# Seven half products for eight on freshly made score groups as well: seven more attention groups per batch on the cheaper scheme

## The chip, the cores and the metric

The kernel runs on one core of a Trainium2 chip. The metric is the device time of one execution in microseconds (us), the median of several runs. The engines are PE (matrix multiply; PEld is its weight load), DVE (vector), ACT (scalar), POOL (general purpose) and SP (issues transfers).

## The reference, cut to what matters

```python
# u, v: 8 x 3008 x 256; z: 8 x 3008 x 64
scores = (1/S) * z @ z.T                # per batch, symmetric
attn   = maximum(scores, 0) ** 2        # still symmetric
x      = u * (attn @ v)
h      = x @ w_in                       # 256 -> 2048
out    = (h * cos(h)) @ w_out           # 2048 -> 256
```

Of the kernel before, what the change touches and what calls it, by code (L numbers as in the profile page):

```python
# [14 lines left out]
def kernel(  # L15
# [9 lines left out]
    nc = tc.nc  # L25
    AF = mybir.ActivationFunctionType
    ALU = mybir.AluOpType
# [20 lines left out]
    NSLOT = 18  # L48
    NW = 4
    PLAN = {  # L50
        2: [(1.0, 'P1 P5'), (1.4, 'P2 B1'), (2.15, 'P6'), (2.55, 'B1'),
            (3.0, 'P3 B1'), (3.4, 'P7'), (4.15, 'B1'), (4.35, 'A1 B1'), (4.75, 'A2'),
            (5.0, 'P4 A1 B1'), (5.4, 'B1'), (6.15, 'A1 B1'), (6.35, 'A1'),
            (6.55, 'A3 B3'), (6.75, 'A3 B1'), (7.0, 'B1'), (7.4, 'A3 B2')],
        3: [(1.0, 'P1 P5 P2'), (2.55, 'P6'), (2.75, 'B2'), (3.0, 'B2'),
            (3.4, 'P3'), (4.15, 'P7'), (4.75, 'A1'), (5.0, 'P4 A1 B1'), (5.4, 'B2'),
            (6.15, 'A1'), (6.35, 'A2'), (6.55, 'A1 B2'), (6.75, 'A2'), (7.0, 'B2'),
            (7.4, 'A3')],
        4: [(0.75, 'P1 P5'), (1.0, 'P2'), (2.35, 'P6 B1'), (2.75, 'P3'),
            (3.4, 'P7'), (4.55, 'B2'), (4.75, 'P4 A1'), (5.0, 'A1 B1'), (5.4, 'A1'),  # L60
            (6.15, 'B1'), (6.35, 'A1'), (6.55, 'A3'), (6.75, 'B1'), (7.0, 'B1')],
        5: [(1.0, 'P1 P5'), (1.4, 'P2'), (2.15, 'P6'), (2.75, 'P3 B1'),
            (3.0, 'B1'), (4.15, 'P7'), (4.35, 'B1'), (4.55, 'A1'), (5.0, 'P4'),
            (5.4, 'B2'), (6.35, 'A1'), (6.55, 'A2 B1'), (7.0, 'A2 B1'), (7.4, 'A1')],
    }
    SUM1, SUM2, WADD, RADD = (-3.0, 0.5), (1.5, 0.15000000000000002), 4.56, 4.25
    CMIN, XEND = 2, 4.0
    HALF = 4.4

    inv_s = 1.0 / float(S)  # L70
    inv_s2 = inv_s * inv_s
# [154 lines left out]
    def direct(b, c, R):  # L226


        return b == 0 and c <= 2

    halves = {}
    slot_of = {}

# [2 lines left out]

    def seven(b, c):

        if c < CMIN or direct(b, c, c):
            return []  # L240
        return list(range(min(c, NW)))

    def s_matmuls(b, c, R, p):


        zt = zT[b % 2]
        banks = {}
        diagonal = R == c and (b, c) > (0, NC // 2)
        for k in ((0, 1), (3, 2) if diagonal else (2, 3))[p]:
            s0 = k if diagonal else 0  # L250
            lo = 1 if k in ((1, 2) if diagonal else (1, 3)) else 0
            h = slice(lo * dqk, (lo + 1) * dqk)
            j0 = c * K + 1 - lo
            sp = ps_w.tile([P, CW], FP32, name="w")
            chain(nc.tensor.matmul(  # L255
                sp[:, s0 * P:], zt[h, R * K + k + 1 - lo, :],
                zt[h, j0 + s0:j0 + K, :].rearrange("p j w -> p (j w)"),
                start=True, stop=True))
            banks[k] = sp
        return banks  # L260

    def s_squares(b, c, R, p, banks):
        if p == 0:
            halves[(b, c, R)] = slot("a", b, c, R)
        t = halves[(b, c, R)]
        diagonal = R == c and (b, c) > (0, NC // 2)
        rt = rpool.tile([P, 2, CW], FP16, name="rt")
        if diagonal:

            for i in range(2):  # L270
                k = 2 * p + i
                nc.scalar.activation(rt[:, i, k * P:], banks[k][:, k * P:], AF.Relu)  # L272
                nc.vector.tensor_tensor(  # L273
                    t[:, k, k:, :].rearrange("p s w -> p (s w)"),
                    rt[:, i, k * P:], rt[:, i, k * P:], ALU.mult)
                if k < K - 1:
                    nc.sync.dma_start_transpose(
                        t[:, k + 1:, k, :],
                        t[:, k, k + 1:, :].rearrange("p s w -> p (s w)"))
            if p == 1:  # L280
                fresh[(b, c, R)] = [t[:, k, :, :] for k in range(K)]
            return
        for i in range(2):
            k = 2 * p + i
            if direct(b, c, R) and (k == 3 or c == R == 0 and i):
                nc.vector.tensor_scalar_max(rt[:, i, :], banks[k], 0.0)
            else:
                nc.scalar.activation(rt[:, i, :], banks[k], AF.Relu)  # L288
        rv = rt.rearrange("p k (s w) -> p k s w", s=K)
        nc.vector.tensor_tensor(  # L290
            t.rearrange("p s k w -> p k s w")[:, 2 * p:2 * p + 2], rv, rv, ALU.mult)
        if p == 1:
            fresh[(b, c, R)] = [t[:, :, k, :] for k in range(K)]
            if R > c and not direct(b, R, c):
                tt = slot("t", b, c, R)
                turned[(b, c, R)] = tt
                nc.sync.dma_start_transpose(
                    tt.rearrange("p s k w -> p (s k) w"),
                    t.rearrange("p s k w -> p (s k w)"))
# [22 lines left out]
    def wide(b, c):  # L322
        return min(CW, S - c * CW)
# [59 lines left out]
        nc.gpsimd.tensor_tensor(o[:, 1], t[:, k2, d2], o[:, 0], ALU.subtract)  # L383
        nc.gpsimd.tensor_tensor(o[:, 3], t[:, k2, d1], o[:, 1], ALU.subtract)

    def quarter(b, c, R, kk, tk):

        h = wide(b, c) // 2
        tt = turned[(b, R, c)].rearrange("p s k w -> p s (k w)")
        return tt[:, 2 * kk:2 * kk + 2, tk * h:(tk + 1) * h]  # L390

    def second(b, c, R):
        h = wide(b, c) // 2
        t = slots[slot_of[("x", b, c)]].rearrange("p (r k h) -> p r k h", r=K, k=2)
        return t[:, R, :, 0:h]

    def a_sums1(b, c, R):
        s1 = quarter(b, c, R, 0, 1)
        after(nc.vector.tensor_tensor(s1, s1, quarter(b, c, R, 1, 1), ALU.add).ins,
              before[-1], NOSYNC)  # L400
        nc.vector.tensor_tensor(
            second(b, c, R), s1, quarter(b, c, R, 0, 0), ALU.subtract)

    def a_sums2(b, c, R):

        h = wide(b, c) // 2
        tt = turned[(b, R, c)].rearrange("p s k w -> p (s k w)")
        part = tt.ap[0]
        src = bass.AP(tt.tensor, tt.offset + 2 * CW,
                      (part, (h, 2), (CW, 2), (1, h)))  # L410
        dst = bass.AP(tt.tensor, tt.offset + h,
                      (part, (2 * CW - h, 2), (CW, 2), (1, h)))
        x = second(b, c, R)
        sub = x.unsqueeze(1).broadcast_to([P, 2, 2, h])
        after(nc.vector.tensor_tensor(dst, src, sub, ALU.subtract).ins,  # L415
              before[-1], NOSYNC)

# [2 lines left out]
    def product(b, c, n):  # L420
# [9 lines left out]
        for i, R in enumerate(W):  # L430
            j = R * K
            v0 = lambda kk, dd: vs(b, j // G)[
                :, j % G + 2 * kk:j % G + 2 * kk + 2, dd * P:(dd + 1) * P]
            lhs, rhs = {
                1: lambda: (v0(0, 0), quarter(b, c, R, 0, 0)),
                2: lambda: (v0(1, 0), quarter(b, c, R, 1, 0)),
                3: lambda: (v0(1, 1), quarter(b, c, R, 0, 1)),
                4: lambda: (vsum[R][:, 3], quarter(b, c, R, 1, 1)),
                5: lambda: (vsum[R][:, 0], quarter(b, c, R, 0, 1)),
                6: lambda: (vsum[R][:, 1], second(b, c, R)),  # L440
                7: lambda: (vsum[R][:, 2], quarter(b, c, R, 1, 0)),
            }[n]()
            for k in range(2):
                chain(nc.tensor.matmul(  # L444
                    acc[bank][:, cols], lhs[:, k, :], rhs[:, k, :],
                    start=(n in (1, 5) and i == k == 0),
                    stop=(i == len(W) - 1 and k == 1), skip_group_check=True))

# [64 lines left out]
    def at(t, rank, f):  # L513
        events.append((t, rank, len(events), f))
# [47 lines left out]
                use(("a", b, c, R), t, t + 3)  # L562
    for b in range(B):
        for R in range(NW):
            at(b * span + (2.0 + 0.5 * R if b else 2 * U + R), 2, lambda b=b, R=R: v_sums(b, R))
        for c in range(NC):
            t = b * span + c * U
            W = seven(b, c)
            d = direct(b, c, c)
            ready = 1.5 + when[(b, c, NC - 1)]  # L570
            first, last = (0.6, 6.93) if d else (HALF if W else 1.0, 7.3)
            room = [i for i, sc in enumerate(scores)
                    if max(ready, t + first) < sc[0] < t + last and i not in also]
            if room:
# [9 lines left out]
                places = [(t + q + (0.5 if q < U - 1 else -0.05), 3) for q in range(U)]  # L584
            elif W:
                for i, R in enumerate(W):
                    at(t + SUM1[0] + SUM1[1] * i, 2, lambda b=b, c=c, R=R: a_sums1(b, c, R))
                    use(("x", b, c), t + SUM1[0], t + XEND)
                    use(("t", b, R, c), t, t + 6.5)
                    at(t + SUM2[0] + SUM2[1] * i, 2.5, lambda b=b, c=c, R=R: a_sums2(b, c, R))  # L590
                at(t + WADD, 2.6, lambda b=b, c=c: keep(b, c, 0))
                at(t + RADD, 2.6, lambda b=b, c=c: keep(b, c, 8))
                done = [0, 0]
                for o, what in PLAN[c]:
                    for piece in what.split():
# [120 lines left out]
```

## The kernel before: the parts that the change and the argument touch

A batch has 24 blocks of 128 keys (the last has 64) and six *columns* of 512 queries (the last has 448). A *group* (c, R) is the attention of the four key blocks R with the queries of column c. As the scores are symmetric, a group with R > c is made once and turned by a transposing transfer for its mirror image. A column's visit takes eight *units*, about 25 us; times in the program are in units from the start of the visit or of the batch. Score matmuls, products with v and the two layers that follow are interleaved on PE by these times.

Plainly, a group costs eight matmuls of 512 columns (four key blocks times two halves of d, the 256 features of v). In the seven-product scheme the group and its v blocks are cut into 2 x 2, and seven products of sums do the work of eight: 14 matmuls of 256 columns. Sums of the attention quarters are made on DVE, sums of the v quarters on POOL, once per batch and key group. In the code, `after(x, y, NOSYNC)` only keeps the scheduler from placing x before y; nothing waits for it.

```python
def v_sums(b, R):                       # POOL; k1, k2: block pairs; d1, d2: halves of d
    o = vsum[R]
    after(nc.gpsimd.tensor_tensor(o[:, 0], t[:, k1, d2], t[:, k1, d1], ALU.subtract).ins, before[-1], NOSYNC)
    nc.gpsimd.tensor_tensor(o[:, 2], t[:, k2, d2], t[:, k1, d2], ALU.subtract)
    nc.gpsimd.tensor_tensor(o[:, 1], t[:, k2, d2], o[:, 0], ALU.subtract)
    nc.gpsimd.tensor_tensor(o[:, 3], t[:, k2, d1], o[:, 1], ALU.subtract)

def a_sums1(b, c, R):                   # DVE, both inputs in SBUF
    s1 = quarter(b, c, R, 0, 1)
    after(nc.vector.tensor_tensor(s1, s1, quarter(b, c, R, 1, 1), ALU.add).ins, before[-1], NOSYNC)
    nc.vector.tensor_tensor(second(b, c, R), s1, quarter(b, c, R, 0, 0), ALU.subtract)
# ... a_sums2: one more subtraction of twice the size, between products 6 and 7

def s_squares(...):                     # DVE, both inputs in SBUF
    nc.scalar.activation(rt[:, i, :], banks[k], AF.Relu)          # empties a PSUM bank
    nc.vector.tensor_tensor(t[...], rv, rv, ALU.mult)             # frees rt
def h_quantum(...):                     # DVE, one input in PSUM, one in SBUF
    nc.vector.tensor_tensor(gs[...], hp, c16, ALU.mult)           # empties a PSUM bank

# when (before):
at(b * span + (2.0 + 0.5 * R if b else 2 * U + R), 2, lambda b=b, R=R: v_sums(b, R))
```

Before, only turned groups (R < c) of columns 2 to 5 used the scheme: 102 groups. Score matmuls and the two layers share six PSUM work banks; PE stops when none is free.

## Time and profile before

| | before |
|---|---|
| time, median of the runs beside the changed kernel | 1231.01 us (1228.36 to 1232.28, 4 runs) |
| span of the profiled run, granted clock | 1230.2 us, 0.999 |
| PE / DVE / ACT / POOL busy | 99% / 77% / 66% / 19% |
| start to start of a matmul of 512 / 256 columns, most frequent | 0.216 / 0.109 us |
| PE time lost (see below) | 22.0 us, of which 13.0 in the first 76 us |

*PE time lost* is used throughout. It was worked out from the order of time of all PE matmuls: the time from one start to the next, less columns/2400 us and 0.0025 us; a run of matmuls of 64 rows counts half its columns, as two run side by side, and each switch between 64 and 128 rows counts 0.09 us (there are 242 of them in every run, so this choice doesn't touch the differences). What is left of the span, 1230.2 - 22.0 = 1208.2 us, is by this construction the time of the columns at full clock: it follows from the number of matmuls.

The page's first part (engine, busy us, share of the span, instructions) of the kernel before:

```profile
PE 1218.0 (99%) x8145; PEld 740.2 (60%) x8145; DVE 941.4 (77%) x1788; ACT 817.3 (66%) x1702; POOL 235.7 (19%) x329
```

From its groups of instructions, shapes kept apart (count | busy us, mean ns | idle before): the first sums on DVE, whose second half is L401, and the squares.

```profile
L290 DVE TENSOR_TENSOR s<-rt 128x1024 f16<-128x1024 f16 x254 | 178.2, 708 | 138.7 <-ACT rt L288 131.9 <-DMA s<-s 5.9
L401 DVE TENSOR_TENSOR s<-s 128x512 f16<-128x512 f16 x70 | 28.8, 420 | 1.0
L399 DVE TENSOR_TENSOR s<-s 128x512 f16<-128x512 f16 x70 | 28.6, 419 | 0.0
```

The order of time around the start of batch 4 (start, duration). First POOL of the kernel before: its v sums run from 594.27 to 602.9 us, one group after the other. Those that need the sum just made start 0.74 to 0.75 us after it, so there is a pause of 0.07 to 0.08 us before each of them (595.83 to 595.91, for one).

```profile
592.15 2.12 POOL L113 DMA_DIRECT2D v<-in_v_dram  x3
594.27 0.82 POOL L380 TENSOR_TENSOR vsum<-v 128x256 f16<-128x256 f16 x1
595.17 0.66 POOL L383 TENSOR_TENSOR vsum<-v,vsum 128x256 f16<-128x256 f16 x1
...
602.27 0.67 POOL L384 TENSOR_TENSOR vsum<-v,vsum 128x256 f16<-128x256 f16 x1
```

DVE of the same kernel in the same stretch: from 594.49 to 604.45 us it has nothing but `g` products, with one input in PSUM, and they keep their 0.69 us.

```profile
594.49 2.48 DVE L484 TENSOR_TENSOR g<-w,c 128x512 f16<-128x512 f32 x4
598.87 0.69 DVE L484 TENSOR_TENSOR g<-w,c 128x512 f16<-128x512 f32 x1 [1.91 <-ACT c L481]
...
604.45 0.69 DVE L290 TENSOR_TENSOR s<-rt 128x1024 f16<-128x1024 f16 x1 [2.28 <-ACT rt L288]
```

### The profile page before, as it was taken

The page shows a single profiled execution, that of the slowest core. Times are in us where ns is not written, and L with a number is a line of the kernel's source. Part 1 is how long each engine was busy: PE and PEld are TensorE (multiplying, and loading weights), DVE is VectorE, ACT ScalarE, POOL GpSimd, SP SyncE. Part 2 cuts the span into 40 slices and gives each one's busy share as a digit, 9 for nine tenths or more (in the row PEclk, how much of TensorE's full clock was granted, in tenths as well). Part 3 has the DMA queues.
Part 4 walks back from the last instruction along what each step waited for, and adds up shares of the span by engine and source line. Part 5 has one row for each costly group of instructions (what it writes and reads, how often), then busy time and mean ns, then how long its engine had stood idle before and what let it go on. Part 6 is the DMA issues. An engine that isn't in the chain of part 4 may idle for free.

```text
span 1230.2 us, 22337 instructions
## 1 busy us (share of the span) xinstructions
PE 1218.0 (99%) x8145; PEld 740.2 (60%) x8145; DVE 941.4 (77%) x1788; ACT 817.3 (66%) x1702; POOL 235.7 (19%) x329
## 2 busy tenths in 40 slices
PE   8999999999999999999999999999999999999998
PEld 3366555665566655666556665566655666556666
DVE  8888767886688866888678886687867878678775
ACT  6667666676676766767667676676766767666645
POOL 5610401014010150101501014010140111400000
PEclk9999999999999999999999999999999999999999
DMA  9997957689696796967969679685795857956411
GB/s 161 172 164 118 145 91 125 116 127 144 96 123 113 118 144 104 123 105 118 147 99 128 101 118 150 100 129 104 111 155 98 131 101 110 158 94 118 72 28 51
DMA packets 484221, 144.97 MB, mean 118 GB/s; under 512 B 432400, under 2 KB 484112, under 8 KB 484112
## 3 DMA queue, kind: packets, MB, share of 16 engines
q1 hardware_dynamic: 356448, 88.73, 45.2%
q0 software_dynamic: 100400, 29.77, 25.5%
q10 hardware_dynamic: 27264, 25.06, 6.4%
q8 instruction: 64, 1.05, 0.4%
q14 instruction: 45, 0.37, 0.1%
HBM read 60.29 MB, written 24.64 MB: 69 GB/s over the span
## 4 chain that ended last, share of the span: by engine, by line
PE 92%; DMA 4%; issue 1%; POOL 1%; DVE 1%; ACT 1%; POOLq 0%; DVEq 0%
PE w L494 25%; PE w L477 25%; PE acc L340 22%; PE acc L444 12%; PE w L255 6%; DMA v<-in_v_dram 4%; DMA ut<-ust 1%; PE acc L317 1%; POOL v L113 1%; POOL vsum L382 0%; DVE g L484 0%; PE w L673 0%; ACT rt L288 0%; ACT zT L218 0%; ACT c L481 0%
## 5 line engine op out<-in xcount | busy, mean ns | idle before, releaser
L481 ACT ACTIVATE c<-w 128x512 f16<-128x512 f32 x752 | 439.1, 623 | 263.3 <-PE w L477 224.8
L484 DVE TENSOR_TENSOR g<-w,c 128x512 f16<-128x512 f32 x752 | 492.4, 685 | 104.0 <-ACT c L481 101.7
L494 PE MATMUL w<-w_out,g 128*128 128x256 f16 x3008 | 448.7, 273 | 0.0
L477 PE MATMUL w<-x,w_in 128*128 128x512 f16 x1504 | 445.9, 379 | 0.0
L494 PEld LDWEIGHTS <-g 128*128 128x128 f16 x3008 | 294.2, 98 | 191.2
L340 PE MATMUL acc<-s,v 128*128 128x512 f16 (+1 forms) x1392 | 363.7, 380 | 2.2 <-DVE x L369 2.2
L288 ACT ACTIVATE rt<-w 128x512 f16<-128x512 f32 x489 | 253.2, 616 | 89.6 <-PE w L255 89.6
L290 DVE TENSOR_TENSOR s<-rt 128x1024 f16<-128x1024 f16 x254 | 178.2, 708 | 138.7 <-ACT rt L288 131.9
L340 PEld LDWEIGHTS <-v 128*128 128x128 f16 x1392 | 130.9, 98 | 130.6 <-issue 36.6
L477 PEld LDWEIGHTS <-w_in 128*128 128x128 f16 x1504 | 146.8, 98 | 66.0 <-issue 4.1
L113 POOL DMA_DIRECT2D ust<-in_u_dram x112 | 81.6, 735 | 527.6 <-PE acc L340 508.8
L444 PE MATMUL acc<-s,vsum 128*128 128x256 f16 (+1 forms) x816 | 106.0, 268 | 0.0
L255 PE MATMUL w<-zT 64*128 64x512 f16 (+3 forms) x684 | 91.6, 361 | 3.6 <-ACT zT L218 1.6
L444 PEld LDWEIGHTS <-vsum 128*128 128x128 f16 x816 | 78.9, 98 | 11.9 <-issue 1.9
L444 PE MATMUL acc<-s,v 128*128 128x256 f16 (+1 forms) x612 | 79.7, 269 | 0.0
L272 ACT ACTIVATE rt<-w 128x512 f16<-128x512 f32 (+3 forms) x176 | 63.0, 451 | 23.9 <-PE w L255 23.9
L501 ACT ACTIVATE ob<-w 128x256 f32<-128x256 f32 x188 | 71.1, 378 | 5.4 <-PE w L494 5.4
L369 DVE TENSOR_TENSOR x<-acc,ut 128x64 f16<-128x64 f32 (+7 forms) x178 | 69.4, 430 | 5.9 <-PE acc L340 3.8
L444 PEld LDWEIGHTS <-v 128*128 128x128 f16 x612 | 57.8, 98 | 13.6 <-issue 8.6
L415 DVE TENSOR_TENSOR s<-s,s 128x1024 f16<-128x1024 f16 (+1 forms) x102 | 63.6, 664 | 2.7 <-PE acc L444 2.7
L273 DVE TENSOR_TENSOR s<-rt 128x512 f16<-128x512 f16 (+3 forms) x176 | 51.0, 340 | 17.9 <-ACT rt L272 17.2
L255 PEld LDWEIGHTS <-zT 64*128 64x128 f16 x684 | 25.6, 94 | 59.8 <-issue 45.7
(38 smaller groups left out, 371.8 us busy)
## 6 DMA issues: line engine op xcount, KB each, us to landing
out_dram<-ob ACTq DMA_DIRECT2D x92, 256.0 KB, 2.3
ust<-in_u_dram POOLq DMA_DIRECT2D x80, 128.0 KB, 5.0
v<-in_v_dram POOLq DMA_DIRECT2D x16, 512.0 KB, 6.5
s<-s SPq DMA_TRANSPOSE x249, 4.6
v<-in_v_dram POOLq DMA_DIRECT2D x8, 448.0 KB, 10.3
zst<-in_z_dram POOLq DMA_DIRECT2D x14, 128.0 KB, 5.0
ust<-in_u_dram POOLq DMA_DIRECT2D x16, 96.0 KB, 4.4
w_in<-in_moe_w_in_dram POOLq DMA_DIRECT2D x4, 256.0 KB, 10.2
```

What stands on the lines that cost most here:

```text
L113: hold(nc.gpsimd.dma_start(dst, src))
L255: chain(nc.tensor.matmul(sp[:, s0 * P:], zt[h, R * K + k + 1 - lo, :], zt[h, j0 + s0:j0 + K, :].rearrange("p j w -> p (j w)"), start=True, ...
L288: nc.scalar.activation(rt[:, i, :], banks[k], AF.Relu)
L290: nc.vector.tensor_tensor(t.rearrange("p s k w -> p k s w")[:, 2 * p:2 * p + 2], rv, rv, ALU.mult)
L340: chain(nc.tensor.matmul(acc[:, 0:wn], vs(b, j // G)[:, j % G, nh * P:(nh + 1) * P], a, start=(start and n == 0), stop=(last and n == len( ...
L369: nc.vector.tensor_tensor(x[:, nh, :], acc[nh][:, o:o + n], ut[:, nh, o:o + n], ALU.mult)
L444: chain(nc.tensor.matmul(acc[bank][:, cols], lhs[:, k, :], rhs[:, k, :], start=(n in (1, 5) and i == k == 0), stop=(i == len(W) - 1 and k ...
L477: chain(nc.tensor.matmul(hp, w_in16[:, k, ft * P:(ft + 1) * P], x[:, k, :], start=(k == 0), stop=(k == NDH - 1)))
L481: nc.scalar.activation(c16, hp, AF.Sin, bias=math.pi / 2.0, scale=inv_s2)
L484: nc.vector.tensor_tensor(gs[(m, ft // FG)][:, ft % FG, :], hp, c16, ALU.mult)
L494: chain(nc.tensor.matmul(ys[m][:, 0:D], gs[(m, f4)][:, ft % FG, ts * P:(ts + 1) * P], w_out16[:, ft, :], start=(ft == 0), stop=(ft == NFT ...
L501: nc.scalar.activation(obs[m][:, i, :], ys[m][:, 0:D], AF.Copy, bias=0.0, scale=inv_s2)
```

## The change

The intent: PE does nothing but stream columns, so use the cheaper scheme for more groups. A fresh group (R > c, or on the diagonal) lies with keys and queries laid out the other way about, so its quarters are found by other strides. In every batch but the first, columns 0 to 3 now have three such groups and columns 4 and 5 four: 151 instead of 102. As column 0 now needs vsum one unit into its visit, the v sums move from 2.0 units after the batch's start to before it.

```diff
-    SUM1, SUM2, WADD, RADD = (-3.0, 0.5), (1.5, 0.15), 4.56, 4.25
-    CMIN, XEND = 2, 4.0
-    HALF = 4.4
+    SUM1, SUM2, WADD, RADD = {0: (-3.9, 0.65), 1: (-3.8, 0.35), ...}, ...
+    TSUM = [-2.0, -1.9, -0.8, 2.0, 2.5]
+    WSET = {0: [0, 1, 2], 1: [0, 1, 2], 2: [0, 1, 2], 3: [0, 1, 2], 4: [0, 1, 2, 3], 5: [0, 1, 2, 3]}
+    HALF = {0: 5.2, 1: 3.9, 2: 3.7, 3: 4.1, 4: 4.2, 5: 4.7}
...   (PLAN: the places of the products within a visit, anew for columns 0 to 5)
     def seven(b, c):
-        if c < CMIN or direct(b, c, c):
-            return []
-        return list(range(min(c, NW)))
+        return [] if direct(b, c, c) else WSET[c]
...   (quarter() becomes quarters(), which takes the strides of either layout)
-                    acc[bank][:, cols], lhs[:, k, :], rhs[:, k, :],
+                    acc[bank][:, cols], lhs[:, k, :],
+                    rhs[:, k, :] if old else rhs[:, :, k * P:(k + 1) * P],
...
-            at(b * span + (2.0 + 0.5 * R if b else 2 * U + R), 2, lambda b=b, R=R: v_sums(b, R))
+            at(b * span + (TSUM[R] if b else 2 * U + R), 2, lambda b=b, R=R: v_sums(b, R))
```

## The prediction

> **What bounds it now.** TensorE. The page shows PE busy 99% of 1230.2 us, granted clock full (0.999), DVE 77%, ACT 66%, and the chain that ended last is 92% PE. Busy is modelled for matmuls, so I read start-to-start spacing in the order of time of the PE instructions: in the steady state a 512-column matmul starts every 0.216 us and a 256-column one every 0.109 us, whatever its line. That is the "N/2.4 + 2.5 ns" of the Trainium skill, "TensorE: Matmul & The Clock Gate", section "Back-to-back issue gap" (215.8 and 109.2 ns); its "sustained" 131 ns for 512 columns is not what this trace shows. Weight loads (98 ns) hide even at 256 columns. PE's time is thus columns plus about 2.5 ns per matmul, plus few stalls. After the first 75 us the only visible ones are waits for the third v load at the start of batches 3 to 5 (chain of waits: DMA v, 4.2 us on PEld in 5 places, 1.9 us on PE, overlapping); by spacing some 2.3 us are lost.
>
> **What the change does.** Groups done with seven half products go from 102 to 151: per batch 1 to 7, column 0 gets 3, column 1 gets 3, column 2 one more (its diagonal). By the instruction order the PE loses 392 matmuls of 512 columns and gains 686 of 256; nothing else on PE changes in number, and the switches between 64-row and 128-row matmuls stay at 242.
> - PE: 392 x 0.216 - 686 x 0.1087 = 84.7 - 74.6 = **-10.1 us**, all on the critical path (0.206 us per group).
> - DVE: 49 x (0.419 + 0.420 + 0.685) for the sums, 14 x (0.424 + 0.414 + 0.690) for combining in the two newly converted columns: +96 us, 941 to about 1037, 85% of the span. ACT: 28 x 0.377 + 14 x 0.413 = +16 us, to about 834. POOL: same operations, issued earlier.
> - The windows of batch 4 show DVE 61% and 69% busy in columns 0 and 1 and 77 to 86% in columns 2 to 5, without PE stalls. After: about 85% to 90% everywhere. So most of the added DVE work lands in idle time.
> - The half-row product of column 0 moves from 1.0 to at least 5.2 eighths of its visit, and the third v group is first read near 6: the v waits should vanish (about -2 us). POOL now makes vsum before that load; it is issued some 2 to 3 us later, harmlessly.
>
> **What is given back.** DVE bursts (three or four 0.685 us subtractions together) delay the evacuations that free the six PSUM work banks, and blocks in bank 0 follow within 0.1 to 0.3 unit of an in-place add. I allow 1 to 2 us for all 48 visits.
>
> Predicted: 1230.9 - 10.1 - 2 + 1 = about **1219.8 us** (0.9% less), 8 times in 10 between 1214.5 and 1226. Chances: faster by over 2% 0.01, within 2% 0.97, slower by over 2% 0.02.
>
> **What would show the steps.** Right: matmul spacing still 0.216 and 0.109; batch period falling from 152.5 to about 151 us; batch 0 unchanged; DVE near 1037 us with per-operation means unchanged; no PE or PEld wait for v after the first batch. Wrong: PE or PEld waits for DVE (acc, x, g, s lines) of over 3 us in total, above all in columns 0 and 1; products waiting for POOL vsum at a batch's start; strided moving operands (two runs of 128) spaced wider than 0.109.
>
> **What would make it wrong.** DVE at 85 to 90% leaves little slack: if each converted visit stalls PE by 0.3 us, 48 visits return the gain entirely. A late vsum of the third group could stall each of seven batches by about 1 us.

## The result, and the profile after

| | before | after |
|---|---|---|
| time, median | 1231.01 us (4 runs) | 1267.33 us (1266.09 to 1268.61, 4 runs) |
| span, granted clock | 1230.2 us, 0.999 | 1266.8 us, 0.980 |
| PE time lost | 22.0 us | 68.3 us |
| span less PE time lost | 1208.2 us | 1198.5 us |

The ratio is 1.0298 (95% interval 1.0278 to 1.0318): 3% slower. Ratios here are the mean time of one kernel's fast runs over that of the other's fast runs of the same rounds, so not quite the ratio of the medians. The last row is worth a look first: the columns, counted at full clock, cost 9.7 us less, as forecast, and 46 us of lost PE time came on top. (That row is a count; what was measured is that the spacing stays at 0.216 and 0.109 us.)

The page after, answering to the line of before:

```profile
PE 1229.4 (97%) x8439; PEld 774.7 (61%) x8439; DVE 1057.0 (83%) x1977; ACT 836.1 (66%) x1744; POOL 237.8 (19%) x329
```

Its groups, shapes apart. L422 and L424 are the two first sums. Before, both took 0.42 us; now the second has a mean of 705 ns. The excess is 119 x (0.705 - 0.417) = 34 us.

```profile
L301 DVE TENSOR_TENSOR s<-rt 128x1024 f16<-128x1024 f16 x254 | 180.4, 717 | 102.3 <-ACT rt L299 101.1
L424 DVE TENSOR_TENSOR s<-s 128x512 f16<-128x512 f16 x119 | 83.3, 705 | 1.5
L422 DVE TENSOR_TENSOR s<-s 128x512 f16<-128x512 f16 x119 | 51.4, 437 | 0.0
```

A mean of this kind asks for the spread. The view of that one line shows a median of 416 ns and a maximum of 6365 ns:

```profile
L424 DVE TENSOR_TENSOR s<-s x151: 377/416/6365, 56.5 to 1213.5; 128x512 f16<-128x512 f16 x119, 128x448 f16<-128x448 f16 x32
```

Looked up in the order of time, seven of the 119 carry the excess: one at each of the seven batch starts, three of about 6.36 us and four of 4.50 us (there POOL's row is shorter: six sums, and a pause before the seventh of 0.33 and 0.50 us in two batches and of 0.01 to 0.02 us in the other two). Here is DVE at the start of batch 3:

```profile
448.93 0.69 DVE L301 TENSOR_TENSOR s<-rt 128x1024 f16<-128x1024 f16 x1
449.54 6.35 DVE L424 TENSOR_TENSOR s<-s 128x512 f16<-128x512 f16 x1
455.81 1.15 DVE L301 TENSOR_TENSOR s<-rt 128x1024 f16<-128x1024 f16 x1
```

And POOL in the same stretch. Nine v sums run from 449.94 to 455.61 us. Those of the first two groups are interleaved, and successive ones start 0.63 us apart, less than the 0.66 us that one takes; the first pause is the 0.07 us before L394 at 455.68, which needs the result of the L391 just before it. L424 ends 0.2 us after that.

```profile
449.94 1.31 POOL L391 TENSOR_TENSOR vsum<-v 128x256 f16<-128x256 f16 x2
451.20 1.29 POOL L394 TENSOR_TENSOR vsum<-v,vsum 128x256 f16<-128x256 f16 x2
...
454.95 0.66 POOL L391 TENSOR_TENSOR vsum<-v 128x256 f16<-128x256 f16 x1
455.68 0.73 POOL L394 TENSOR_TENSOR vsum<-v,vsum 128x256 f16<-128x256 f16 x1
```

PE after: its last matmul before the stall starts at 452.79; then it finds no free work bank for its scores, because DVE, stuck at L424, does not empty them.

```profile
452.79 0.39 PE L263 MATMUL w<-zT 64*128 64x512 f16 x1
457.62 0.48 PE L263 MATMUL w<-zT 64*128 64x384 f16 x1 [4.44 <-DVE g L506]
```

The stall has a second price. The windows view after (the last columns are the granted clock, the share of the DMA engines and GB/s) shows half the clock from 456 us on; in the trace's clock records it lasts 6.8 us, and matmuls of 512 columns then start 0.43 us apart.

```profile
451.00:456.00 5.00, 2.18 (x14) 1.04 (x12) 5.00 (x2) 0.54 (x1) 4.92 (x9) 1.00 1.49 128
456.00:459.00 3.00, 0.93 (x4) 0.31 (x4) 3.00 (x5) 0.89 (x3) 3.00 (x5) 0.50 0.90 132
459.00:462.50 3.50, 3.50 (x12) 1.23 (x10) 3.22 (x10) 2.99 (x7) 2.49 (x4) 0.50 1.24 162
```

The Trainium skill, "TensorE: Matmul & The Clock Gate", Part 1, says that the array's clock drops to half after at least one idle window of about 3.4 us, until it has been busy for as long. This trace agrees in the lengths: after the start of the kernel, the seven stretches at half clock last 3.4, 6.8 or 10.2 us. But the idle time was often shorter: in four of the seven the longest gap before the drop was 2.1 to 2.6 us, and PE was busy for up to 1.9 of the 3.4 us before it. After the first 76 us, the columns that were started at half clock account for 17 of the 46 us; the rest is waiting.

The theory, **A**: an instruction of DVE with both inputs in SBUF cannot run while POOL runs one that reads SBUF, and waits until POOL pauses. The Trainium skill, "SBUF — State Buffer", section "Who interferes with whom", states the first half: such a DVE instruction "contends with a GpSimd instruction that reads SBUF, not with one that only writes it", as its second input comes through a read port that the two share, held as an exclusive lock. The narrower form **A'**: only an operation caught at the start of the run is starved; others lose one POOL instruction at most (about 0.46 us, as seen elsewhere in the trace). The rival, **B**: the subtraction is slow by itself, by its addresses, or because transposing transfers write nearby, and POOL's run beside it is a coincidence. The whole trace of the changed kernel leans to A: of the 56 DVE tensor operations with two SBUF inputs that overlap POOL's sums, 44 take over 0.15 us more than the median of their form; of 827 that do not overlap them, one does; of 65 that overlap them with an input in PSUM, none.

### The profile page after: what moved, and what is told of

It reads as the page before. It is cut to its first block, busy times and chain, and to the rows that moved or that the text cites. A ratio compares the mean times of both kernels' runs of the same rounds, so it can differ in the third digit from the quotient of the medians.

```text
span 1266.8 us, 23106 instructions
## 1 busy us (share of the span) xinstructions
PE 1229.4 (97%) x8439; PEld 774.7 (61%) x8439; DVE 1057.0 (83%) x1977; ACT 836.1 (66%) x1744; POOL 237.8 (19%) x329
## 4 chain that ended last, share of the span: by engine, by line
PE 90%; DVE 7%; ACT 1%; issue 1%; DMA 1%; DVEq 0%
PE w L516 25%; PE w L499 25%; PE acc L465 18%; PE acc L351 15%; PE w L263 6%; DVE s L424 3%; DVE g L506 1%; DVE s L301 1%; DMA ut<-ust 1%; ACT rt L299 1%; PE acc L328 1%; DVE s L422 0%; PE w L695 0%; ACT zT L224 0%; DVE x L380 0%
## 5 line engine op out<-in xcount | busy, mean ns | idle before, releaser
L516 PE MATMUL w<-w_out,g 128*128 128x256 f16 x3008 | 454.9, 275 | 0.0
L499 PE MATMUL w<-x,w_in 128*128 128x512 f16 x1504 | 453.9, 385 | 0.0
L351 PE MATMUL acc<-s,v 128*128 128x512 f16 (+1 forms) x1000 | 284.9, 381 | 2.5 <-DVE x L380 2.5
L465 PE MATMUL acc<-s,vsum 128*128 128x256 f16 (+1 forms) x1208 | 157.9, 270 | 0.9 <-DVE q L481 0.5
L351 PEld LDWEIGHTS <-v 128*128 128x128 f16 x1000 | 93.2, 98 | 86.8 <-issue 37.3
L263 PE MATMUL w<-zT 64*128 64x512 f16 (+3 forms) x684 | 101.0, 367 | 29.7 <-DVE g L506 26.3
L465 PEld LDWEIGHTS <-vsum 128*128 128x128 f16 x1208 | 117.2, 98 | 17.9 <-issue 4.4
L465 PE MATMUL acc<-s,v 128*128 128x256 f16 (+1 forms) x906 | 117.6, 270 | 0.0
L434 DVE TENSOR_TENSOR s<-s,s 128x1024 f16<-128x1024 f16 (+1 forms) x151 | 95.0, 671 | 9.3 <-PE acc L465 8.9
L465 PEld LDWEIGHTS <-v 128*128 128x128 f16 x906 | 85.4, 98 | 20.4 <-issue 12.4
L424 DVE TENSOR_TENSOR s<-s 128x512 f16<-128x512 f16 (+1 forms) x151 | 95.6, 638 | 2.0
L263 PEld LDWEIGHTS <-zT 64*128 64x128 f16 x684 | 26.3, 94 | 87.3 <-issue 73.4
```

The lines of the kernel that those rows point to most:

```text
L263: chain(nc.tensor.matmul(sp[:, s0 * P:], zt[h, R * K + k + 1 - lo, :], zt[h, j0 + s0:j0 + K, :].rearrange("p j w -> p (j w)"), start=True, ...
L351: chain(nc.tensor.matmul(acc[:, 0:wn], vs(b, j // G)[:, j % G, nh * P:(nh + 1) * P], a, start=(start and n == 0), stop=(last and n == len( ...
L424: nc.vector.tensor_tensor(second(b, c, R), s1, quarters(b, c, R, (0, 0)), ALU.subtract)
L434: after(nc.vector.tensor_tensor(dst, src, sub, ALU.subtract).ins, before[-1], NOSYNC)
L465: chain(nc.tensor.matmul(acc[bank][:, cols], lhs[:, k, :], rhs[:, k, :] if old else rhs[:, :, k * P:(k + 1) * P], start=(n in (1, 5) and i ...
L499: chain(nc.tensor.matmul(hp, w_in16[:, k, ft * P:(ft + 1) * P], x[:, k, :], start=(k == 0), stop=(k == NDH - 1)))
```

## The experiments

| run | v sums | time, median us | ratio to before | PE time lost us |
|---|---|---|---|---|
| after | POOL, interleaved, -2.0 on | 1267.33 | 1.0298 | 68.3 |
| e1_sums_early | the same, first sums moved away | 1274.67 | 1.0361 | 73.5 |
| e2_vsum_dve | DVE | 1227.76 | 0.9983 | 27.5 |
| e3_before_tsum | kernel before, new moments | 1230.85 | 1.0005 | 21.1 |
| e4_vsum_in_turn | POOL, one group after the other | 1239.30 | 1.0078 | 40.1 |
| e5 / e12 (wrong values) | POOL writes only | 1219.63 / 1218.47 | - / 0.9908 | 18.9 / 19.0 |
| e6_dve_early | DVE, earlier | 1247.28 | 1.0144 | 46.4 |
| e8_spaced | POOL, one at a time | 1244.04 | 1.0125 | 43.5 |
| e9_before_dve | kernel before, DVE | 1265.34 | 1.0290 | 54.3 |
| e10_each_when_free | POOL, spread over two visits | 1229.01 | 0.9996 | 28.4 |
| e11 (wrong values) | DVE, spread | 1227.95 | 0.9992 | 26.2 |
| e13_best | POOL, spread, mended | 1221.42 | 0.9937 | 21.5 |

The 95% intervals of the ratios are about 0.002 to either side.

### e1_sums_early: the slow subtraction moved out of POOL's run

```diff
-    SUM1, ... = {0: (-3.9, 0.65), ...
+    SUM1, ... = {0: (-5.6, 0.65), ...
```

> The changed kernel with the first sums of column 0 (the subtraction that took 4.5 to 6.4 us once per batch) moved from -3.9 to -5.6 eighths of a visit, so that they end before POOL's run of v sums starts; POOL untouched. Theory A (POOL's reads of SBUF hold back any DVE operation with two inputs in SBUF until POOL pauses): the squares of the score groups, also two SBUF inputs, fall into the same run and inherit the wait; one operation per batch stays 4 to 6 us long, 1250 to 1270 us. Theory A' (only an operation that already waits when the run starts is starved, squares lose about 0.5 us each as elsewhere in the trace): 1218 to 1226 us. Rival B (the subtraction itself is slow, by its addresses or by transposes into neighbouring slots, whatever POOL does): it is as long at its new place, 1260 to 1270 us, and it is this line that is long, not the squares.

Measured: 1274.67 us. The subtraction is back to a median of 417 ns with a maximum of 894. At all seven batch starts the wait went to a square of another line, shape and place (three of 6.25 us, four of 4.4). DVE of this run:

```profile
450.30 0.69 DVE L301 TENSOR_TENSOR s<-rt 128x1024 f16<-128x1024 f16 x1 [0.29 <-ACT rt L299]
451.28 6.25 DVE L301 TENSOR_TENSOR s<-rt 128x1024 f16<-128x1024 f16 x1 [0.29 <-ACT rt L299]
457.45 2.47 DVE L506 TENSOR_TENSOR g<-w,c 128x512 f16<-128x512 f32 x4
```

POOL of the same run: its back-to-back sums start at 451.31, and the first pause comes between 456.98 and 457.05.

```profile
451.31 1.31 POOL L391 TENSOR_TENSOR vsum<-v 128x256 f16<-128x256 f16 x2
...
456.32 0.66 POOL L391 TENSOR_TENSOR vsum<-v 128x256 f16<-128x256 f16 x1
457.05 1.00 POOL L394 TENSOR_TENSOR vsum<-v,vsum 128x256 f16<-128x256 f16 x1
```

Theory A holds and B falls: it is not this subtraction. A' is not decided here, since the square, too, is recorded just as POOL's run starts (451.28 and 451.31); e3 decides it. The kernel became slower than the changed kernel, and beyond the expected range, because the moved sums now delay an in-place addition (L484) for which products of column 5 wait: up to 1.8 us on PE once per batch.

### e2_vsum_dve: no POOL arithmetic

```diff
-        nc.gpsimd.tensor_tensor(o[:, 0], ...)      # all four
+        nc.vector.tensor_tensor(o[:, 0], ...)
```

> The changed kernel with the v sums on DVE instead of POOL: no POOL arithmetic after the start, the subtraction at its place. Theory A: no DVE operation over 1.3 us, the subtraction's mean back to 0.42 us, about 30 to 40 us more DVE work for 128 more operations of some 0.28 us, time 1216 to 1228 us. Rival B: the subtraction stays 4.5 to 6.4 us long once per batch, 1265 to 1275 us.

Measured: 1227.76 us, so 39.6 us off the changed kernel's median by this one edit. The subtraction stays where it was and has a mean of 420 ns. The run is at the slow end of what was expected: PE still loses 1.2 us at each batch start, where ten v sums stand on DVE close to the squares.

### e3_before_tsum: the kernel before, with the new moments alone

```diff
-            at(b * span + (2.0 + 0.5 * R if b else 2 * U + R), ...
+            at(b * span + ([-2.0, -1.9, -0.8, 2.0][R] if b else 2 * U + R), ...
```

> The kernel before with nothing but the new moments of the v sums (-2.0, -1.9, -0.8, 2.0 instead of 2.0, 2.5, 3.0, 3.5). Its own first sums stand elsewhere, so only squares can meet POOL's run. Theory A: the squares wait 3 to 6 us per batch, 1245 to 1265 us. Theory A': squares lose about 0.5 us each, 1228 to 1234 us. Rival B: no change, 1229 to 1233 us.

Measured: 1230.85 us, unchanged. This is a miss for A as I had put it, and the trace tells why. DVE of this run:

```profile
587.40 2.22 DVE L290 TENSOR_TENSOR s<-rt 128x1024 f16<-128x1024 f16 x2 [0.29 <-ACT rt L288]
589.54 2.47 DVE L484 TENSOR_TENSOR g<-w,c 128x512 f16<-128x512 f32 x4
591.93 0.67 DVE L369 TENSOR_TENSOR x<-acc,ut 128x192 f16<-128x192 f32 x2
592.53 2.28 DVE L273 TENSOR_TENSOR s<-rt 128x512 f16<-128x512 f16 x1
```

POOL's run starts at 588.24; its first pause is the one after 594.53:

```profile
593.87 0.66 POOL L380 TENSOR_TENSOR vsum<-v 128x256 f16<-128x256 f16 x1
594.61 0.73 POOL L383 TENSOR_TENSOR vsum<-v,vsum 128x256 f16<-128x256 f16 x1
```

Without the extra sums, DVE is early enough to get its squares in at the start of it (POOL's first pair takes 1.90 instead of 1.29 us: here, it seems, POOL waited). Then come six operations with an input in PSUM, which keep their times. Only the square at 592.53 meets the run, near its end, and waits 1.9 us. That settles A': the square came in the middle of the run, not at its start, and waited for three POOL instructions until the pause; so it was in all seven batches. DVE makes it good with little loss on PE (some 0.5 us per batch). So the move of the v sums alone costs nothing, and the half products alone cost nothing that PE feels (e12): it is the two together, the run and a DVE operation with two SBUF inputs at its beginning.

### e4_vsum_in_turn: the same POOL work, with pauses

```diff
+        ops = [o[:, 2], o[:, 0], o[:, 1], o[:, 3]]      # the last two need the one before
+        for a in ops:
+            if pooled: after(a.ins, pooled.pop(), NOSYNC)   # order on POOL only, no wait
+            pooled.append(a.ins)
```

> The changed kernel with POOL's v sums in the order of one group after the other, each two that depend on each other side by side, instead of two groups interleaved: POOL then starts a dependent operation 0.75 us after the one before instead of 0.63 us, which leaves a gap of some 0.07 us. Theory A with release in the gaps: the subtraction gets in at the first gap and takes at most about 2 us; time 1219 to 1230 us. Theory A without it (DVE waits for the end of the whole run): 6 us long as before, 1262 to 1270 us. Rival B: 1265 to 1270 us.

Measured: 1239.30 us; the longest subtraction is 2034 ns:

```profile
L430 DVE TENSOR_TENSOR s<-s x151: 381/418/2034, 56.0 to 1185.3; 128x512 f16<-128x512 f16 x119, 128x448 f16<-128x448 f16 x32
```

An instruction that needs its predecessor's result starts 0.75 us after it instead of 0.63; DVE gets in there. The same 16 operations at nearly the same time: 28 us less (medians of different rounds). The wait ends at POOL's first pause, not at the end of its work. The time is above the range expected, as squares that follow are caught too (0.46 us each).

### e5_write_only and e12_write_only_timed: POOL busy, but not reading

```diff
-    (four gpsimd.tensor_tensor per group)
+    for n in (0, 2, 1, 3):
+        for half in range(3): nc.gpsimd.memset(o[:, n], 0.01 * (half + 1))
```

> Wrong results on purpose: the changed kernel with every POOL v sum replaced by three POOL memsets of the same tile, so that POOL is busy at the same moments and writes SBUF, but reads nothing. Theory A as the SBUF page of the Trainium skill words it (the clash is over reading): no DVE operation over 1.3 us at the batch starts, the subtraction back to 0.42 us, 1215 to 1228 us. Theory A with any POOL access to SBUF: the subtraction is held back for as long as the memsets run back to back, over 2 us once per batch.

> Wrong results on purpose: e5_write_only again, the same kernel, now timed in rounds against the kernel before. 1217 to 1222 us, ratio 0.990 to 0.994: the time that the half products give when POOL's reads hold nothing back, which is what the prediction had forecast (1219.8 us).

Measured: 1219.63 us in one look (state unknown for a single run), 1218.47 us in rounds, ratio 0.9908 (0.9888 to 0.9928). In the trace of e12, 109 DVE operations with two SBUF inputs overlap POOL's memsets, by 50 us in all, and none takes over 0.01 us more than the median of its form. For example, the two first sums beside a row of memsets:

```profile
575.20 3.09 POOL L389 MEMSET vsum<- 128x256 f16 x12 [1.43 <-PE acc L461]
576.05 0.41 DVE L418 TENSOR_TENSOR s<-s 128x512 f16<-128x512 f16 x1
576.69 0.41 DVE L420 TENSOR_TENSOR s<-s 128x512 f16<-128x512 f16 x1
```

So POOL's reading matters, not its being busy. The limits of this control: the rows of memsets are shorter (12 in 3.1 us; 49 of the 109 meet such a row), and they come at other moments, as they wait for no load of v. The run also gives what the half products are worth undisturbed: 11.2 us by the medians of its rounds, where 11.1 were forecast.

### e6_dve_early and e9_before_dve: the sums on DVE at other places

```diff
 e6 (on e2):      -    TSUM = [-2.0, -1.9, -0.8, 2.0, 2.5]    +    TSUM = [-3.2, -3.1, -0.8, 2.0, 2.5]
 e9 (on before):  -    nc.gpsimd.tensor_tensor(o[...]         +    nc.vector.tensor_tensor(o[...]
```

> The kernel with the v sums on DVE (e2_vsum_dve, 1227.8 us), and the sums of the first two groups moved from -2.0 and -1.9 to -3.2 and -3.1 eighths of a visit. In e2_vsum_dve PE still loses 1.2 us at each batch start, where six of the v sums stand among the squares that free the work banks. If that is the cause: 0.3 to 0.8 us per batch come back, 1222 to 1226 us. If the cause is the total of DVE work there: 1227 to 1229 us.

> The kernel before with nothing but its v sums on DVE (128 operations of about 0.28 us, some 31 us at start-to-start spacing of 0.20 us). DVE is 77% busy there, so the work should hide: 1228 to 1233 us. It is the base against which the half products alone (e2_vsum_dve) can be judged: predicted -10 us if PE has no new stalls, so if this run is near 1230 and e2_vsum_dve 1227.8, about 7 us of the gain are lost in stalls that have nothing to do with POOL.

Both missed: 1247.28 and 1265.34 us. In neither does any operation take longer than it should. DVE of e9:

```profile
601.72 0.69 DVE L290 TENSOR_TENSOR s<-rt 128x1024 f16<-128x1024 f16 x1 [0.29 <-ACT rt L288]
606.06 0.49 DVE L382 TENSOR_TENSOR vsum<-v 128x256 f16<-128x256 f16 x2 [3.66 <-DMA v<-in_v_dram]
606.47 0.69 DVE L290 TENSOR_TENSOR s<-rt 128x1024 f16<-128x1024 f16 x1
```

In these traces DVE takes its operations in their order. A sum placed before its v load has landed stops DVE, and with it the squares and evacuations behind it: 3.66 us here, 2.09 us in e6. The scheduler had put these two sums (L382, which no `after` ties to a place) between the squares. So e9 is no base for e2, as I had meant it to be; and on POOL, idle in any case, the same wait had been free (16.0 us in the kernel before).

### e8_spaced: POOL, one sum at a time

```diff
+                for i in range(4):
+                    o = (-3.2, -2.0, -0.7, 2.0)[R] + 0.3 * i
+                    at(b * span + o, 2, ... v_sums(b, R, [i]))   # each waits for its place in PE's order (SYNC)
```

> The changed kernel with the v sums on POOL, but one at a time: each of the 16 of a batch waits for its own place in PE's order, 0.3 eighths of a visit (about 0.95 us) apart, starting at -3.2, so that POOL pauses after every one. Theory A with release in the gaps: no DVE operation is held back longer than one or two POOL operations (0.7 to 1.3 us), PE stalls at the batch start of at most 1 us, 1217 to 1226 us, faster than with the sums on DVE. If gaps do not matter, only the amount of POOL work (same 16 operations): 1245 to 1270 us.

Measured: 1244.04 us, a miss. After batch 0 no single wait is longer than 1.2 us, as expected, and most are near 0.5 us, but they come in a row. (In batch 0, whose sums still follow each other, one square waits 3.3 us.) The POOL sums had stood behind a load in POOL's order, and once it was issued they followed each other again; DVE now gets in after every one of them, and waits for the next. DVE of this run, each operation 0.46 us over its 0.42 or 0.69:

```profile
751.14 0.89 DVE L423 TENSOR_TENSOR s<-s 128x512 f16<-128x512 f16 x1
751.95 1.15 DVE L301 TENSOR_TENSOR s<-rt 128x1024 f16<-128x1024 f16 x1
753.02 0.88 DVE L425 TENSOR_TENSOR s<-s 128x512 f16<-128x512 f16 x1
```

PE loses 1.9 to 4.5 us around each batch start, most in the first three. A pause between POOL's operations limits a wait; it does not make the sum of waits small when the queue of DVE is full.

### e10_each_when_free, e11_dve_when_free, e13_best: each sum at its own place

A part of vsum is free as soon as the old batch's product that reads it is done, and needed only by its own product. So the 16 sums of a batch can be spread over two visits:

```diff
+   o = {0: (-6.7, -5.3, -4.55, -3.2), 1: (-6.5, -5.05, -4.3, -2.95),
+        2: (-0.6, 0.6, 0.9, 2.7), 3: (8.7, 9.0, 10.6, 10.9)}[R][i]      # e10, POOL; e11: DVE, -0.6 -> 0.8
+   o = {0: (-6.7, -5.3, -4.55, 2.6), 1: (-5.5, -5.05, -4.3, 2.75),
+        2: (-0.9, 0.6, 0.9, 2.9), 3: (8.7, 9.0, 10.6, 10.9)}[R][i]      # e13, POOL; batch 0 on DVE
```

> The changed kernel, v sums on POOL, each of the 16 per batch at its own place as soon as the old batch's product has read the part of vsum that it overwrites: the first two groups' sums at -6.7 to -2.95 eighths (during column 5 of the batch before), those of the third group from -0.6 to 2.7, those of the fourth, which only column 4 needs, from 8.7; placed between the bursts of squares that follow a visit of scores, and held to PE's order. Theory A: DVE operations lose at most 0.5 us here and there and no longer in one burst; PE loses under 0.5 us per batch start; 1218 to 1223 us, close to the 1219.6 us of the run in which POOL only wrote, and faster than the kernel before by 0.5% to 1%. If the loss depends on the amount of POOL reading alone: 1235 to 1250 us.

> The same places as e10_each_when_free (third group's first sum at 0.8 instead of -0.6, after its load has landed), but on DVE. No clash with POOL is possible; DVE carries 26 us more by start-to-start spacing, 4 to 5 us of the 25 us around a batch start no longer in one place. Expected 1219 to 1226 us if DVE does not wait for a load of v; with waits of DVE for v as in e6_dve_early and e9_before_dve (2 to 3.7 us per batch), 1240 us or more.

> An attempt to beat both kernels, built from e10_each_when_free by three moves: in the first batch the v sums stand on DVE (there e10_each_when_free lost 7 us around 51 to 58 us, e11_dve_when_free under 3), the last sums of the first two groups go from -3.2 to 2.6 eighths, away from the squares at 740 to 742 us of that trace, and the first sum of the third group goes ahead of the third load of v, to -0.9. If the remaining 1 us of PE stalls per batch start came from those last collisions: 0.3 to 0.6 us per batch, 1213 to 1219 us, ratio 0.986 to 0.992. If not: 1221 to 1226 us.

Measured: e10 1229.01 us, e11 1227.95 us, e13 1221.42 us. The e10 run missed its range: the batch starts behave (0.7 to 1.0 us lost), but about 7 us went in batch 0 between 51 and 58 us, after the same clash again: a square waited 5.8 us beside nine POOL sums; and in each later batch several DVE operations still lost up to 0.7 us beside a sum. The e11 run has wrong values by my mistake: at 0.8 the third group's first sum stands after the second, which needs it. At each batch start it loses 1.7 us. In e13 both faults of e10 are mended; PE loses some 0.6 us at each batch start after the first, two operations per batch are held back by some 0.5 us. Its POOL at a batch start:

```profile
740.18 0.79 POOL L392 TENSOR_TENSOR vsum<-v 128x256 f16<-128x256 f16 x1 [4.04 <-PE acc L351]
740.92 2.12 POOL L119 DMA_DIRECT2D v<-in_v_dram  x3
743.39 0.66 POOL L393 TENSOR_TENSOR vsum<-v,vsum 128x256 f16<-128x256 f16 x1 [0.35 <-PE w L501]
744.02 0.66 POOL L394 TENSOR_TENSOR vsum<-v 128x256 f16<-128x256 f16 x1
749.84 1.92 POOL L395 TENSOR_TENSOR vsum<-v,vsum 128x256 f16<-128x256 f16 x3 [5.16 <-PE w L501]
```

The e13 version is correct and beats both kernels: ratio 0.9937 to the kernel before (0.9921 to 0.9953), which is clear of the noise, and 45.9 us below the changed kernel by the medians of their own rounds. It is slower than I expected (1213 to 1219 us); of its 21.5 us lost, 14.0 lie in the first 76 us, which is batch 0 filling up, and were not studied further.

## Why the prediction was right or wrong, point by point

- **"PE: -10.1 us, all on the critical path": right.** Spacing stayed at 0.216 and 0.109 us, also for the moving operands of two runs of 128, so the count of matmuls gives 9.7 us less; and e12, with the clash taken away, is 11.2 us faster than the kernel before.
- **"The v waits should vanish": right.** Neither PE nor PEld waits for v after the first batch in the changed kernel.
- **"ACT to about 834": right** (836.1; 834.2 in e12). **"DVE to about 1037": off both ways.** It is 1057.0 with the operations that were held back, and 1008.4 undisturbed (e12). I added durations, but back-to-back operations overlap in the records: 0.42 us long, they start 0.33 us apart.
- **"POOL: same operations, issued earlier": this is the step that failed, and with it "I allow 1 to 2 us".** The step put the cost of POOL's move at nothing; PE lost 46 us more. I had looked only at whether POOL's results come in time. What its reads do to DVE, a wait between engines, was not in the sum. In the kernel before, the v sums ran beside DVE operations with an input in PSUM, and with short pauses; the change moved them to where DVE has squares and sums with both inputs in SBUF, and interleaved them into one row without pause. One such operation per batch then waited 4.1 to 5.9 us more than its median of 0.42, PE stood for up to 4.8 us from start to start, and ran at half clock for a while after that (17 of the 46 us). Shown by e1 (the wait passes to another operation), e2 and e12 (it goes when POOL does not read) and e4 (it ends at POOL's first pause). "Most of the added DVE work lands in idle time" was right by itself: in e12, with the same DVE operations, PE loses 19.0 us, less than the 22.0 before.
- **"What would show the steps wrong" named the right place but not the cause.** PE's waits for DVE at batch starts, "over 3 us in total", is what the trace shows (26.3 us for a work bank). "DVE at 85 to 90% leaves little slack" may be part of it, which no run shows by itself: e3 fits, with the same collision, shorter and later in POOL's run, absorbed by the kernel before.
- **The time**: forecast 1219.8 us, measured 1267.33. With POOL's reads out of the way it is 1218.47 us (e12), within the range forecast. The arithmetic was right for a kernel in which the engines do not meet.

## What to carry to other kernels

When a change moves work of an engine that is hardly busy, ask what it will then run beside, not only whether it comes in time: list for POOL's new stretch the DVE operations whose inputs both lie in SBUF. Keep POOL's reading instructions apart from those, or at least apart from one another, since one that follows another without pause holds DVE off for the whole row. And when a group's mean goes up while its median stays, look for the few long ones and for what all of them have beside them.

## What the Trainium skill lacked or had wrong

- "SBUF — State Buffer", "Who interferes with whom", has the clash itself, and the runs agree: DVE with two SBUF inputs is held back by POOL's reads, while operations with one input in PSUM keep 0.69 us beside the same POOL run, and memsets do nothing (109 overlapping operations, none over 0.01 us longer than its median). What it lacks is that a DVE operation does not get in between two POOL instructions that follow without pause (starts 0.63 us apart): it waited 5.9 us across nine of them, until a gap of 0.07 us; and a square that came in the middle of such a row (e3) waited 1.9 us. A POOL instruction that needs its predecessor's result opens such a gap (starts 0.75 us apart).
- The same section says that the order of issue decides who blocks. By recorded starts this could not be read off: the DVE operation recorded at 449.54 us, its predecessor ending at 449.62, lost to a POOL run recorded from 449.94 on.
- "TensorE: Matmul & The Clock Gate", "Back-to-back issue gap", gives a sustained 131 ns per matmul of 512 columns; all runs here show 216 ns, which is the formula that the section calls isolated (215.8 ns).
